# A transformer block and its gradients: one ScalarE step for two PSUM banks, and a new lead at the start

## The chip, the cores and the metric

The kernel runs on one core of one Trainium2 chip. The metric is the device time of one execution in microseconds (us). The time before is the median of three runs, 581.6 us (581.47 to 582.85). One more execution was taken with the hardware profiler; all rows of the profile come from that one.

The engines are TensorE (PE in the rows; its weight loads are PEld), VectorE (DVE), ScalarE (ACT), GpSimd (POOL) and SyncE (SP, which here issues most DMAs). Matmul results land in PSUM, which this kernel uses as eight banks of 128 partitions by 512 floats. ScalarE and VectorE take results from there to SBUF.

## The reference, cut

One block with attention and a feed-forward part, forward and backward (2048 rows, width 512, 32 heads of 16, 8 keys per row at every second position, 1792 hidden units; everything bf16). Outputs are the block's result and the gradients of x, wqkv, wo, w1, b1, w2 and b2.

```python
def _A_ref(x, wqkv, wo):                       # S=2048, D=512, H=32, Dh=16
    qkv = (x @ wqkv).reshape(B, S, 3, H, Dh).transpose(2, 0, 3, 1, 4)
    q, k, v = qkv[0], qkv[1], qkv[2]
    idx = arange(S)[:, None] - (arange(8) * 2)[None, :]      # 8 keys back, every second
    kg, vg = k[:, :, idx], v[:, :, idx]                      # [B, H, S, 8, Dh]
    logits = where(idx >= 0, einsum("bhsd,bhswd->bhsw", q, kg) * Dh ** -0.5, -1e9)
    o = einsum("bhsw,bhswd->bhsd", softmax(logits), vg)
    return o.transpose(0, 2, 1, 3).reshape(B, S, D) @ wo

def _B_ref(x, w1, b1, w2, b2):
    return gelu(x @ w1 + b1) @ w2 + b2                       # tanh form of gelu

h   = x + _A_ref(layernorm(x), wqkv, wo)
out = h + _B_ref(layernorm(h), w1, b1, w2, b2)
# outputs: out, and vjp(grad_out) for x, wqkv, wo, w1, b1, w2, b2
```

## The kernel before, in words

The 2048 rows are worked in four chunks of 512. For each chunk there are stages: `p1_ln` (first layer norm and its transposed copy `ln1T`), `p1_qkv` (projections, L804 and L821), `p1_attn` (logits and softmax), `p1_o` (attention output), `p1_h` (output projection and second norm), `p2_h`, `p2_out`, `p2_dg`, `p2_bwd` (feed-forward part, forward and backward), `p3_go`, `p3_dots`, `p3_bands`, `p3_gl1` (attention backward). At the end `wg_ffn` makes the weight gradients (L1201), sixteen accumulated matmuls for each, evicted by ScalarE and stored in pairs.

**How the order is set.** Every operation is recorded with its engine, what it reads and what it writes. A list written out in the file, `TURN`, then gives the order in which all 2029 operations are issued, and with it the order on each engine and each DMA queue. A second list, `HOMES`, gives each of the 969 buffers its PSUM bank or SBUF address. Estimated times in the code played a part only in making these lists. A real wait comes from data, or from a buffer whose place an earlier one still holds.

**The band.** The sum over the eight keys is done by `band` (L692 to L714), 64 times: in `p1_o` for the output (`ost`) and in `p3_bands` for the gradients of q, v and k (`gqs`, `gvs`, `gks`). A *pair* is two bands, m = 0 and 1. VectorE multiplies gathered rows (`R`, fetched by GpSimd's indirect DMA, L661) with transposed coefficients (`cf`, L687) into a product of 128x4096 (L698). TensorE sums it with eight matmuls into one PSUM bank (`bs`, at most two at a time, L707). ScalarE takes the bank to SBUF, turned from (d, h) to (h, d) order (L712, called *sink*). When both bands of a pair are there, `unperm` (L716 to L722) transposes the two on TensorE and ScalarE evicts the result (L564).

**The start.** x arrives in four loads of 128 rows, then weights and other chunks. `spin` (L1283) issues matmuls of zeros, eleven at the start and four behind the first transposes, `WARM = (11, 4)`. b1, 1792 biases, is loaded as 14 rows of 128 (`b1b`), turned by one TensorE transpose (`b1t`, L1306) and copied by VectorE to `b1c` (L1307). The biases are used much later by `xb` (L958). VectorE's row statistics (L577, L578), the factor `rstd` from GpSimd (L585) and `nm` (L586) give the norm (L596). The first chunk's norm is done in two halves, each followed by eight transposes (`to_fm_pairs`, L628) and one ScalarE copy. Then come the projections for k and q (two evictions each) and the first products (L672).

**Around 150 to 160 us.** ScalarE there does `xb` (L958, takes h·w1 from PSUM and adds b1), `gelu` (L961) and the squares of the gelu derivative `x2` (L976), for chunks 0 and 1 side by side, and sinks of chunk 1's and 2's attention output.

Of the kernel before, what the change touches and what calls it, by code (L numbers as in the profile page):

```python
# [427 lines left out]
def kernel(  # L428
# [114 lines left out]
    def tt_us(n, f32=False):  # L543
        return 0.16 + (1.04e-3 if f32 else 0.52e-3) * n
# [147 lines left out]
    def band(cf, R, sc, m, sgn, dst, at, sca, tag):  # L692
        pr = sb("prb" + tag, [P, 2, 4, 512], tag="prod", lim=4)
        o0 = (2 if sgn < 0 else 0) + 4 * m
        st = -1024 if sgn < 0 else 1024

        def prod():
            V.tensor_tensor(out=pr().rearrange("p a j (d h) -> p a j d h", h=H),  # L698
                            in0=_sub(R()[:, o0, 0:1], [[st, 2], [512, 4], [32, DH], [1, H]]),
                            in1=_sub(cf()[:, 2 * sc + m, 0, 0, 0:1], [[128, 2], [32, 4], [0, DH], [1, H]]), op=ALU.mult)  # L700
        op("DVE", tt_us(4096), prod, r=[R, cf], w=[pr], tag="prod" + tag)
        ps = ps_("bs" + tag, 1, "bs", 2)

        def sums():
            for hf in range(2):
                for j in range(4):
                    T.matmul(ps()[32 * j:32 * j + 32, :], lhsT=S32[:], rhs=pr()[:, hf, j, :], start=(hf == 0), stop=(hf == 1),  # L707
                             skip_group_check=True)
        op("PE", 0.45, sums, r=[CST, pr], w=[ps], tag="bsum" + tag, al=[dst])

        def out():
            A.activation(out=dst()[:, at, :].rearrange("p (h d) -> p h d", d=DH), in_=ps().rearrange("p (d h) -> p h d", h=H),  # L712
                         func=ACT.Copy, scale=sca)
        op("ACT", act_us(512), out, r=[ps], w=[(dst, at)], tag="sink" + tag)  # L714
# [71 lines left out]
    def p1_ln(c):  # L786
        xt = st_[c]["xt"]
        ln1 = sb("ln1_%d" % c, [P, TPC, D], tag="ln1", lim=L1LIM)
        layernorm(c, xt, MV1, ST1, VE1, NM1, R1, mv1, st1, ve1, nm1, rstd1, ln1, N1[c], TPC if c else 2)
        store(ln1_d[c], lambda: ln1_d[c]()[:].rearrange("(j p) d -> p j d", p=P), ln1, lambda: ln1(), 512, tag="ln1st")  # L790
        ln1T = st_[c]["ln1T"] = sb("ln1T%d" % c, [P, DC, CH], tag="ln1T", lim=L1LIM)
        (to_fm_dma if c in FM1 else to_fm if c else to_fm_pairs)(ln1, ln1T, "ln1")
        if c == 0 and WARM and WARM[1]:
            op("PE", 0.216 * WARM[1], lambda: spin(WARM[1]), r=[wz], w=[wp], tag="warm2", after=[(ln1, 3)])

# [101 lines left out]
    def p1_o(c):  # L897
# [5 lines left out]
        for sc in range(2):  # L903
            for m in range(2):
                band(cf, Rs[sc], sc, m, -1, ost, 2 * sc + m, 1.0, "o")
            unperm(ost, 2 * sc, oT, 0, sc, sc, "o")
# [226 lines left out]
    def p3_bands(c, kind):  # L1133
# [16 lines left out]
        for sc in range(2):  # L1150
            R = gather(src, sc, sgn < 0, kind, after=[(d["got"], 0)] if kind == "q" else [(cf, 0)])
            gs = sb("g%ss" % kind, [P, 2, 512], tag="gs" if c < KEEP else None, lim=4)
            for m in range(2):
                band(cf, R, sc, m, sgn, gs, m, sca, kind)
# [150 lines left out]
    pb = ps_("pb1")  # L1305
    op("PE", 0.1, lambda: T.transpose(pb.bf()[:, 0:FT], b1b[:], ident[0:FT, 0:FT]), r=[B1B], w=[pb], tag="b1t")  # L1306
    op("DVE", 0.2, lambda: V.tensor_copy(out=b1c[:], in_=pb.bf()[:, 0:FT]), r=[pb], w=[B1C], tag="b1c")  # L1307
# [216 lines left out]
N2D = ()  # L1524
B2PE = ()
GB2PE = ()
WARM = (11, 4)
GWA = ()
B1PE = ()
MD = ()  # L1530
# [44 lines left out]
```

## Time and profile before

| | us |
|---|---|
| median of three runs | 581.6 (581.47 to 582.85) |
| profiled execution | 582.24 |
| its span | 580.5 |
| mean granted TensorE clock | 0.997 |
| TensorE busy | 556.8 (96%) |
| TensorE weight loads | 261.3 (45%) |
| VectorE busy | 490.2 (84%) |
| ScalarE busy | 351.6 (61%), 517 instructions |
| GpSimd busy | 90.4 (16%) |
| ScalarE steps of band (L712), 64 in all | 592 to 606 ns each |

The span is the time between the first and the last instruction in the trace; the execution's own time has 1.74 us more. Shares of busy time are averages over the whole span; the stages differ, so the table by stage in the prediction says more. A row of the timeline reads: start, length, engine, line, operation, output and inputs by the program's names, shape, number of instructions, and in brackets how long the engine was idle before and what released it.

### The profile page before, as it was taken

How to read it: one execution, taken by the hardware profiler on the slowest of the kernel's cores; microseconds unless marked ns; L12 is line 12 of the kernel's file. 1: busy time of each engine (PE TensorE's matmuls, PEld its weight loads, DVE VectorE, ACT ScalarE, POOL GpSimd, SP SyncE). 2: the span in 40 equal slices, each digit the busy share in tenths (PEclk: the TensorE clock that was granted, in tenths of full speed). 3: DMA queues.
4: the chain of work that ended last, by engine and by line, in shares of the span. 5: the costliest groups of instructions: out<-in, count | busy, mean ns of one | idle time of the engine just before them, and what ended most of it. 6: DMA issues, size and time to landing. Idle time of an engine off the chain costs nothing.

```text
span 580.5 us, 9212 instructions
## 1 busy us (share of the span) xinstructions
PE 556.8 (96%) x3525; PEld 261.3 (45%) x3579; DVE 490.2 (84%) x645; ACT 351.6 (61%) x517; POOL 90.4 (16%) x89
## 2 busy tenths in 40 slices
PE   7999989799899999999999999999999899999997
PEld 3454544244344444444545444444444446444443
DVE  7999799999999999789865999998998899973900
ACT  5588899998997885988453424136542455364111
POOL 3020605031000000000000100432421241400000
PEclk8999999999999999999999999999999999999999
DMA  8579699999999998989999989989989996879322
GB/s 256 148 254 322 230 260 355 250 189 299 227 260 269 244 279 131 258 239 273 282 233 273 324 298 283 311 316 292 345 342 314 322 311 244 313 235 362 114 73 72
DMA packets 163147, 150.99 MB, mean 260 GB/s; under 512 B 112768, under 2 KB 149536, under 8 KB 158240
## 3 DMA queue, kind: packets, MB, share of 16 engines
q1 hardware_dynamic: 156768, 103.22, 64.1%
q0 software_dynamic: 6336, 47.19, 23.1%
q8 instruction: 28, 0.46, 0.3%
q14 instruction: 15, 0.12, 0.1%
HBM read 78.25 MB, written 42.77 MB: 208 GB/s over the span
## 4 chain that ended last, share of the span: by engine, by line
PE 75%; issue 4%; DVE 4%; ACT 3%; DMA 2%; SPq 0%; ACTq 0%; DVEq 0%
PE ps L1201 25%; PE ps L1060 8%; PE ps L1012 8%; PE ps L1173 7%; PE ps L1037 7%; PE ps L956 6%; PE ps L707 4%; PE ps L1082 2%; PE ps L722 2%; DMA gk_d<-gks 1%; PE ps L679 1%; DVE prbo L698 1%; PE ps L918 1%; ACT xb L958 1%; PE ps L650 1%
## 5 line engine op out<-in xcount | busy, mean ns | idle before, releaser
L956 PE MATMUL ps<-ln2T,w 128*128 128x512 bf16 x224 | 53.5, 379 | 2.5 <-ACT xb L958 2.3
L1037 PE MATMUL ps<-goT,w2T 128*128 128x512 bf16 x215 | 54.1, 379 | 0.4
L1012 PE MATMUL ps<-w,gl 128*128 128x512 bf16 x217 | 51.9, 379 | 0.9 <-ACT xb L958 0.6
L1201 PE MATMUL ps<-gw1in,ln2b 128*128 128x512 bf16 (+1 forms) x256 | 52.6, 353 | 0.0
L1060 PE MATMUL ps<-w1T,xb 128*128 128x512 bf16 x220 | 50.6, 379 | 0.2
L1201 PE MATMUL ps<-gor,gw2in 128*128 128x512 bf16 x217 | 50.2, 379 | 0.4 <-issue 0.2
L1039 DVE SCALAR_TENSOR_TENSOR xb<-xb,ps 128x512 bf16<-128x512 bf16 x56 | 37.9, 683 | 14.6 <-PE ps L1037 13.6
L1173 PE MATMUL ps<-wqkvT,gqkvT 128*128 128x512 bf16 x184 | 42.7, 379 | 0.6 <-issue 0.3
L958 ACT ACTIVATE xb<-ps,b1c 128x512 bf16<-128x512 f32 x56 | 36.7, 686 | 7.3 <-PE ps L956 7.2
L698 DVE TENSOR_TENSOR prbk<-Rk,cfk 128x4096 bf16<-128x4096 bf16 x16 | 36.0, 2288 | 6.0 <-DMA Rk<-q_d,rowi 2.7
L564 ACT CAST wgs<-ps 128x512 bf16<-128x512 f32 (+1 forms) x30 | 16.6, 559 | 38.8 <-PE ps L1201 38.7
L698 DVE TENSOR_TENSOR prbv<-Rv,cfv 128x4096 bf16<-128x4096 bf16 x16 | 36.3, 2287 | 3.3 <-PE ps L1201 1.8
L698 DVE TENSOR_TENSOR prbq<-Rq,cfq 128x4096 bf16<-128x4096 bf16 x16 | 36.3, 2278 | 2.3 <-PE ps L707 0.8
L672 DVE TENSOR_TENSOR prf<-qt,kt 128x4096 bf16<-128x4096 bf16 x16 | 35.9, 2278 | 1.4 <-PE ps L707 0.7
L672 DVE TENSOR_TENSOR prb<-got,vw 128x4096 bf16<-128x4096 bf16 x16 | 36.1, 2280 | 1.2 <-DMA vw<-v_d 0.6
L698 DVE TENSOR_TENSOR prbo<-Ro,cfo 128x4096 bf16<-128x4096 bf16 x16 | 36.2, 2286 | 0.3
L661 POOL DMA_INDIRECT Rq<-k_d,rowi x8 | 15.5, 1940 | 130.2 <-PE ps L1012 103.4
L737 ACT ACTIVATE gyr<-ps,rstd 128x512 bf16<-128x512 f32 x32 | 21.9, 685 | 21.5 <-PE ps L1173 18.5
L1201 PEld LDWEIGHTS <-ln2b 128*128 128x128 bf16 x256 | 24.0, 98 | 23.8 <-issue 3.4
L956 PEld LDWEIGHTS <-w 128*128 128x128 bf16 x224 | 21.1, 98 | 29.9 <-issue 5.6
L980 ACT ACTIVATE xb<-xb 128x2048 bf16<-128x2048 bf16 (+1 forms) x16 | 27.1, 1695 | 11.9 <-DVE xb L979 11.9
L1201 PEld LDWEIGHTS <-gw2in 128*128 128x128 bf16 x224 | 21.2, 98 | 27.4 <-issue 3.4
(178 smaller groups left out, 1069.8 us busy)
## 6 DMA issues: line engine op xcount, KB each, us to landing
g_d<-xrg SPq DMA_DIRECT2D x12, 512.0 KB
gh_d<-xrh SPq DMA_DIRECT2D x12, 512.0 KB
gw2in<-g_d SPq DMA_DIRECT2D x3, 2048.0 KB
gw1in<-gh_d SPq DMA_DIRECT2D x3, 2048.0 KB
ln_d<-ln SPq DMA_DIRECT2D x8, 512.0 KB
w<-in_B_w_dram SPq DMA_DIRECT2D x2, 1792.0 KB
out_dram<-wgs SPq DMA_DIRECT2D x13, 256.0 KB
v_d<-tmv SPq DMA_DIRECT2D x8, 256.0 KB
```

What stands on the lines that cost most here:

```text
L672: op("DVE", tt_us(4096), lambda g=g, pr=pr: V.tensor_tensor(out=pr(), in0=ql()[:, g, :].unsqueeze(1).to_broadcast([P, W, 512]), in1=_sub(k ...
L698: V.tensor_tensor(out=pr().rearrange("p a j (d h) -> p a j d h", h=H), in0=_sub(R()[:, o0, 0:1], [[st, 2], [512, 4], [32, DH], [1, H]]), i ...
L707: T.matmul(ps()[32 * j:32 * j + 32, :], lhsT=S32[:], rhs=pr()[:, hf, j, :], start=(hf == 0), stop=(hf == 1), skip_group_check=True)
L956: T.matmul(ps(), lhsT=w1()[:, dc, f * P:(f + 1) * P], rhs=cols(ln2T[c], dc, c in FM2), start=(dc == 0), stop=(dc == DC - 1))
L958: op("ACT", act_us(512, 1), lambda f=f, ps=ps, xb=xb, f0=f0: A.activation(out=xb()[:, f - f0, :], in_=ps(), func=ACT.Identity, bias=b1c[:, ...
L980: op("ACT", act_us(N), lambda xb=xb: A.activation(out=fl(xb), in_=fl(xb), func=ACT.Tanh, scale=GC), w=[xb], tag="tanh", mode=2)
L1012: T.matmul(ps(), lhsT=d["g"][f // 4]()[:, f % 4, j * P:(j + 1) * P], rhs=w2()[:, f, :], start=(f == 0), stop=(f == FT - 1))
L1037: T.matmul(ps(), lhsT=w2T()[:, dc, f * P:(f + 1) * P], rhs=goT()[:, dc, :], start=(dc == 0), stop=(dc == DC - 1))
L1039: op("DVE", 0.70, lambda f=f, ps=ps, z=z, f0=f0: V.scalar_tensor_tensor(out=z()[:, f - f0, :], in0=z()[:, f - f0, :], scalar=1.0, in1=ps() ...
L1060: T.matmul(ps(), lhsT=d["d"][f // 4]()[:, f % 4, j * P:(j + 1) * P], rhs=w1T()[:, f, :], start=(f == 0), stop=(f == FT - 1))
L1173: T.matmul(ps(), lhsT=d["gqkv"]()[:, b, j * P:(j + 1) * P], rhs=wqkvT()[:, b, :], start=(i == 0 and b == ks[0]), stop=(i == 2 and b == ks[ ...
L1201: T.matmul(ps()[:, 0:N], lhsT=l, rhs=r, start=(n == 0), stop=(n == k - 1))
```

## The change

Four things change together.

1. `band` becomes `bands`, which does a whole pair. The two products and the two groups of sums stay as they are, each sum in a PSUM bank of its own (at most two, as before). One ScalarE step of 128x1024 then takes both banks; the distance between the banks is a stride in its address pattern, so they need not be neighbours. 64 sinks become 32.
2. `b1t` and `b1c` are no longer recorded ahead of everything but in `p1_ln` of chunk 0, behind `ln1T`. The first rows' transposes now stand ahead of them.
3. `WARM` is (18, 4): seven more matmuls of zeros at the start.
4. `TURN` and `HOMES` are new as a whole (1997 operations). The stages follow one another as before. Most operations move by two or three us against their neighbours, some by up to 30. The weights of k are loaded ahead of those of q, q's first half is evicted ahead of k's, `b1t` stands behind six groups of projection matmuls and `b1c` ahead of the first product. Of the two squares (L976) that stood together near 153 us, one is now ahead of an earlier `gelu` and one behind a later one. At the end three pairs of rows are evicted and stored close together.

The diff, without the two lists:

```diff
-    def band(cf, R, sc, m, sgn, dst, at, sca, tag):
-        pr = sb("prb" + tag, [P, 2, 4, 512], tag="prod", lim=4)
...
+    def bands(cf, R, sc, sgn, dst, at, sca, tag):
+
+        two = []
+        for m in range(2):
+            pr = sb("prb" + tag, [P, 2, 4, 512], tag="prod", lim=4)
...
+            op("DVE", tt_us(4096), prod, r=[R, cf], w=[pr], tag="prod" + tag)
+
+            ps = ps_("bs" + tag, 1, "bs", 2)
+            two.append(ps)
...
+            op("PE", 0.45, sums, r=[CST, pr], w=[ps], tag="bsum" + tag, al=[dst])
 
         def out():
-            A.activation(out=dst()[:, at, :].rearrange("p (h d) -> p h d", d=DH), in_=ps().rearrange("p (d h) -> p h d", h=H),
-                         func=ACT.Copy, scale=sca)
-        op("ACT", act_us(512), out, r=[ps], w=[(dst, at)], tag="sink" + tag)
+            p0, p1 = two
+            A.activation(out=dst()[:, at:at + 2, :].rearrange("p m (h d) -> p m h d", d=DH),
+                         in_=_sub(p0(), [[(p1.home - p0.home) * BANK, 2], [1, H], [H, DH]]), func=ACT.Copy, scale=sca)
+        op("ACT", act_us(1024), out, r=two, w=[(dst, at), (dst, at + 1)], tag="sink" + tag)
...
+        if c == 0:
+            pb = ps_("pb1")
+            op("PE", 0.1, lambda: T.transpose(pb.bf()[:, 0:FT], b1b[:], ident[0:FT, 0:FT]), r=[B1B], w=[pb], tag="b1t", after=[(ln1T, None)])
+            op("DVE", 0.2, lambda: V.tensor_copy(out=b1c[:], in_=pb.bf()[:, 0:FT]), r=[pb], w=[B1C], tag="b1c")
...
-            for m in range(2):
-                band(cf, Rs[sc], sc, m, -1, ost, 2 * sc + m, 1.0, "o")
+            bands(cf, Rs[sc], sc, -1, ost, 2 * sc, 1.0, "o")
...
-            for m in range(2):
-                band(cf, R, sc, m, sgn, gs, m, sca, kind)
+            bands(cf, R, sc, sgn, gs, 0, sca, kind)
...
-    pb = ps_("pb1")
-    op("PE", 0.1, lambda: T.transpose(pb.bf()[:, 0:FT], b1b[:], ident[0:FT, 0:FT]), r=[B1B], w=[pb], tag="b1t")
-    op("DVE", 0.2, lambda: V.tensor_copy(out=b1c[:], in_=pb.bf()[:, 0:FT]), r=[pb], w=[B1C], tag="b1c")
...
-WARM = (11, 4)
+WARM = (18, 4)
```

More of the change, by code (lines that the diff above doesn't have):

```diff
@@ L690, in coefs, with prod, sums @@
         return cf
-    def band(cf, R, sc, m, sgn, dst, at, sca, tag):
-        pr = sb("prb" + tag, [P, 2, 4, 512], tag="prod", lim=4)
[L694 to L709, printed above, removed]
+    def bands(cf, R, sc, sgn, dst, at, sca, tag):
+        two = []
+        for m in range(2):
+            pr = sb("prb" + tag, [P, 2, 4, 512], tag="prod", lim=4)
+            o0 = (2 if sgn < 0 else 0) + 4 * m
+            st = -1024 if sgn < 0 else 1024
+            def prod(pr=pr, o0=o0, m=m):
+                V.tensor_tensor(out=pr().rearrange("p a j (d h) -> p a j d h", h=H),
+                                in0=_sub(R()[:, o0, 0:1], [[st, 2], [512, 4], [32, DH], [1, H]]),
+                                in1=_sub(cf()[:, 2 * sc + m, 0, 0, 0:1], [[128, 2], [32, 4], [0, DH], [1, H]]), op=ALU.mult)
+            op("DVE", tt_us(4096), prod, r=[R, cf], w=[pr], tag="prod" + tag)
+            ps = ps_("bs" + tag, 1, "bs", 2)
+            two.append(ps)
+            def sums(pr=pr, ps=ps):
+                for hf in range(2):
+                    for j in range(4):
+                        T.matmul(ps()[32 * j:32 * j + 32, :], lhsT=S32[:], rhs=pr()[:, hf, j, :], start=(hf == 0), stop=(hf == 1),
+                                 skip_group_check=True)
+            op("PE", 0.45, sums, r=[CST, pr], w=[ps], tag="bsum" + tag, al=[dst])
```

250 rows, old and new, of tables (HOMES, TURN) are left out of this document.

## The prediction

> **What bounds the kernel now.** I read the table of busy time by stage first, then the waits of TensorE, then the chain that ended last, then the timeline where those point.
>
> The first view is the windows table: stretch in us, its length, then busy time and count of instructions of PE, PEld, DVE, ACT and POOL, the granted clock, the DMA share and GB/s.
>
> ```profile
> 0.00:12.00 12.00, 7.77 (x33) 3.69 (x34) 8.66 (x30) 6.74 (x18) 3.98 (x22) 0.86 0.79 244
> 12.00:50.00 38.00, 37.45 (x274) 18.32 (x277) 36.47 (x53) 26.06 (x29) 5.23 (x5) 1.00 0.73 227
> ...
> 134.00:160.00 26.00, 22.99 (x117) 10.27 (x119) 25.31 (x47) 23.94 (x28) 2.52 (x2) 1.00 1.00 243
> 160.00:440.00 280.00, 278.27 (x1658) 129.39 (x1683) 248.53 (x335) 161.96 (x237) 33.71 (x28) 1.00 0.96 278
> 440.00:480.00 40.00, 37.96 (x290) 17.43 (x284) 34.59 (x22) 18.70 (x33) 14.20 (x10) 1.00 0.92 313
> 480.00:575.00 95.00, 93.86 (x591) 46.40 (x594) 58.04 (x77) 34.60 (x76) 9.40 (x4) 1.00 0.59 207
> 575.00:580.50 5.50, 1.83 (x9) 0.63 (x7) 0.00 (x0) 0.59 (x1) 0.00 (x0) 1.00 0.27 92
> ```
>
> From 160 to 440 TensorE is busy for 278.27 of 280 us: there only TensorE work counts, and the change removes none of it. Before 160 three engines are nearly full at once: VectorE has 36.47 of 38, and from 134 to 160 it has 25.31 of 26 beside ScalarE's 23.94, while TensorE has holes. Time is to be had in four places: the start, the stretch before 160, 440 to 480, and the end.
>
> The second view is TensorE's longest sum of waits (what waits, releaser: us in total, times, the longest); the third is the chain that ended last, by engine.
>
> ```profile
> PE ps L707 <- DVE prbo L698: 5.0, 6, 1.6
> ```
> ```profile
> PE 75%; issue 4%; DVE 4%; ACT 3%; DMA 2%; SPq 0%; ACTq 0%; DVEq 0%
> ```
>
> The sums over a band (L707) wait for VectorE's product, not for the ScalarE step that this change merges. ScalarE has 3% of the chain, so the 32 steps less are worth little by their number.
>
> **Part one: the start.** Timeline rows (start, length, engine, line; in brackets the idle time before and its releaser) of TensorE, VectorE and ScalarE, then the first projections and products, warm transposes, and the clock:
>
> ```profile
> 1.87 3.97 PE L1283 MATMUL ps<-wz 128*128 128x512 bf16 x11 [1.87 <-DVE wz L1284]
> 7.38 0.18 PE L1306 MATMUL ps<-ident,b1b 14*128 14x14 bf16 x1 [1.54 <-POOL rstd L585]
> 8.34 2.20 PE L628 MATMUL ps<-ident,ln 128*128 128x128 bf16 x16 [0.78 <-DVE ln L596]
> 10.33 1.66 PE L1283 MATMUL ps<-wz 128*128 128x512 bf16 x4
> ```
> ```profile
> 6.53 0.09 DVE L831 MEMSET kt<- 128x32 uint32 x1
> 7.59 0.17 DVE L1307 CAST b1c<-ps 128x14 f32<-128x14 bf16 x1 [0.98 <-PE ps L1306]
> 7.68 0.15 DVE L586 SCALAR_TENSOR_TENSOR nm<-mv,rstd 128x2 f32<-128x2 f32 x1
> ```
> ```profile
> 11.67 0.18 DVE L578 BATCH_NORM_AGGREGATE mv<-st 128x2 f32<-128x6 f32 x1
> 11.77 0.66 DVE L577 BATCH_NORM_STATS2 st<-xt 128x6 f32<-128x512 bf16 x1
> ```
> ```profile
> 9.62 1.96 ACT L564 COPY ln1T<-ps 128x1024 bf16<-128x1024 bf16 x2 [3.35 <-PE ps L628]
> ```
> ```profile
> 11.83 7.07 PE L804 MATMUL ps<-ln1T,wqk 128*128 128x512 bf16 x31
> ...
> 16.53 8.90 DVE L672 TENSOR_TENSOR prf<-qt,kt 128x4096 bf16<-128x4096 bf16 x4 [0.61 <-ACT qt L564]
> ...
> 33.99 1.06 PE L615 MATMUL ps<-ident,ln 128*128 128x128 bf16 x16
> ```
> ```profile
> 10.00:12.00 2.00, 2.00 (x11) 0.99 (x9) 1.90 (x7) 1.58 (x2) 0.00 (x0) 0.60 1.08 364
> ```
>
> VectorE stands idle 0.98 us because the copy of the bias vector (b1c) is ahead of the scaled mean (nm) in its order, and it waits for the transpose of that vector, which waits for its load. With both moved behind, nm can start when the memset is over, 6.53 + 0.09 = 6.62, or about 6.65: 7.68 − 6.65 = 1.03 us earlier. The first two rows' norms then let TensorE start its transposes at 8.34 − 1.03 = 7.31.
>
> The seven added matmuls of zeros stand right there. The first eleven end at 1.87 + 3.97 = 5.84. If the later seven take what the 31 projection matmuls take on a warm array, 7.07 / 31 = 0.228 each, they end at 5.84 + 1.6 = 7.4, just when the transposes are due, and cost nothing. If they run at half the clock, 0.46 each, they end near 9.0 and are late by 1.6.
>
> The sixteen transposes took 2.20 us where sixteen warm ones took 1.06, and the granted clock from 10 to 12 is 0.60: after the gap from 5.84 to 8.34 with one small transpose in it, TensorE had lost its clock. With zeros up to 7.4 it keeps it. So the second half of the transposes ends near 9.0 (its norms end 1.03 earlier, near 8.4, and eight warm transposes are half of 1.06), ScalarE's second copy ends near 10.2, against 9.62 + 1.96 = 11.58, and the projections start near 10.4 against 11.83. Not all of that 1.4 reaches VectorE: the moved transpose of the bias vector now follows six groups of four projection matmuls (24 × 0.228 = 5.5), and its copy is ahead of the first product on VectorE. So the first product starts near 10.4 + 5.5 + 0.2 + 0.2 = 16.3 instead of 16.53. But one pass of row statistics more (0.66 + 0.18 = 0.84) is already done ahead of it, so VectorE's work is 0.25 + 0.84 = 1.1 ahead. I take −1.1. The ends: −1.4 if VectorE follows the projections fully; −0.4 if the zeros run at half clock (projections near 11.1, product near 17.0, less the 0.84). The new order loads k's weights before q's and evicts q before k; the product needs both, so I put this at nothing. If a weight load came late here, its 512 KB would cost up to the 1.4 gained.
>
> Should the transposes stay at 2.20 for another cause than the clock, their second half would end 0.5 later, the term would be −0.6 and the forecast 580.2, inside the forecast's own range. The Trainium skill, "TensorE: Matmul & The Clock Gate", section "What's actually happening", speaks for that: it has the array throttled after an idle window of about 3.4 us, and the gap here is 2.5 us. The rows show a clock of 0.60 behind the gap, so I go by them.
>
> **Part two: one ScalarE step for two.** Means of single steps (busy us, mean ns), and two queues of such steps back to back:
>
> ```profile
> L712 ACT ACTIVATE ost<-ps 128x512 bf16<-128x512 f32 x16 | 9.2, 592 | 0.9 <-PE ps L707 0.8
> ```
> ```profile
> L564 ACT CAST tmv<-ps 128x1024 bf16<-128x1024 f32 x8 | 8.0, 1016 | 1.7 <-PE ps L821 1.7
> ```
> ```profile
> L958 ACT ACTIVATE xb<-ps,b1c 128x512 bf16<-128x512 f32 x56 | 36.7, 686 | 7.3 <-PE ps L956 7.2
> ```
> ```profile
> 112.30 1.55 ACT L712 ACTIVATE ost<-ps 128x512 bf16<-128x512 f32 x3
> ```
>
> Nothing here evicts two banks with this permutation in one step; the nearest is the strided 128x1024 eviction at 1016 ns. By means a pair saves 2 × 592 − 1016 = 168 ns. But steps that queue overlap: three took 1.55, so they start (1.55 − 0.59) / 2 = 0.48 apart, two occupy 0.96, and the merged one some 0.93: 0.03 saved. Of the 32 pairs only those before 160 lie where ScalarE is full; there are six. So the term is between 6 × 0.03 = 0.2 and 6 × 0.168 = 1.0; I take −0.5. The other 26 lie under TensorE's 278.27 of 280, where ScalarE has 161.96.
>
> **Part three: the new order around 150 to 160.**
>
> ```profile
> 153.24 2.84 ACT L976 ACTIVATE x<-xb 128x1024 bf16<-128x1024 bf16 x2
> ```
> ```profile
> 156.70 1.02 PE L956 MATMUL ps<-ln2T,w 128*128 128x512 bf16 x4 [2.35 <-ACT xb L958]
> 157.65 0.61 PE L707 MATMUL ps<-prbo,S 128*32 128x512 bf16 x8
> 158.20 1.04 PE L1037 MATMUL ps<-goT,w2T 128*128 128x512 bf16 x3
> 159.80 1.46 PE L1012 MATMUL ps<-w,gl 128*128 128x512 bf16 x6 [0.56 <-ACT xb L958]
> ```
>
> Two squares, 2.84 us, stand on ScalarE ahead of an eviction for which TensorE waits 2.35, and 0.56 more follow. In the new order one square comes before an earlier gelu and the other behind a later one. If the stall goes entirely, 2.35 + 0.56 = 2.9 are won; but the squares still have to be done on a ScalarE that is full, so mostly the stall moves to other steps. I take −0.6, nearer to none; the ends are 0 and −2.9.
>
> **Part four: 440 to 480, and the end.**
>
> ```profile
> 458.17 4.49 DVE L698 TENSOR_TENSOR prbk<-Rk,cfk 128x4096 bf16<-128x4096 bf16 x2 [2.74 <-DMA Rk<-q_d,rowi]
> ...
> 462.58 2.11 DVE L687 STREAM_TRANSPOSE cfv<-shv 128x512 bf16<-128x512 bf16 x2
> 462.71 1.05 PE L707 MATMUL ps<-prbk,S 128*32 128x512 bf16 x16 [1.66 <-DVE prbk L698]
> ```
> ```profile
> 576.87 0.59 ACT L564 CAST wgsq<-ps 128x512 bf16<-128x512 f32 x1 [2.87 <-PE ps L1201]
> ```
>
> VectorE waits 2.74 for a gather before two products. The new order fills part of that with a transpose (2.11 / 2 = 1.06), but TensorE's two sums then follow each other with less between: best −1.1, worst the 1.66 wait grown by a third, +0.6; I take +0.2. At the end one eviction (0.59) and one store follow the last matmuls now; in the new order three pairs of rows are evicted and stored close together: 0 to one eviction and a little more, +0.7; I take +0.1.
>
> **The rest.** The order and the addresses of the other buffers are new, mostly by two or three us either way. Between 160 and 440 TensorE's own work covers that (1.73 us idle of 280); if that cover went, a per cent of it would be 2.8. I put it at nothing.
>
> Sum: −1.1 − 0.5 − 0.6 + 0.2 + 0.1 = −1.9 against the profiled execution's 582.24 (span 580.5 and 1.74 around it), so 580.3. That execution lies 0.64 above the median of the runs shown; carried to the median 581.6 it is **579.7**. What can be told from no change is 0.3%, 1.74 us: faster is below 579.86, slower above 583.34.
>
> **Rivals.** First, the whole stall goes: part three is worth 2.9, so −1.9 − 2.3 = −4.2, 577.4. For it: the 2.35 is one wait with one cause. Against: ScalarE's 23.94 of 26.
>
> Second, slower: the merged step holds both banks. The limit of two banks for these sums is unchanged. Before, the first half's bank was free and half of the pair evicted while VectorE made the second product; now both banks stay occupied until one step of 1.016 after the second sums, and the next pair's sums and this pair's transposes (L722) wait behind it. By the written order about half of the 32 pairs have one or two groups of four matmuls (4 × 0.228 = 0.91 each) between the second sums and those transposes. The merged step needs 1.016 and some 0.2 on either side of it for the handovers, 1.4. With nothing ahead on ScalarE and two groups it fits; it decides where a bias eviction (0.686) stands ahead: 0.686 + 1.016 + 0.2 − 1.5 = 0.4. At 12 such pairs this is 4.8 us of TensorE time where nothing hides it: −1.9 + 4.8 = +2.9, 584.5. For it: TensorE has 278.27 of 280, so every wait there counts. Against: TensorE's waits now hold almost none on the old step. The Trainium skill, "PSUM — Partial Sum Buffer", section "Summary: rules for kernel authors", asks to evacuate promptly, which speaks against this change in the same way; no run here shows a price for it yet.
>
> Third, nothing: the lead of the start is lost where VectorE and ScalarE are both full (134 to 160), and the stall only changes its place: −0.1 to −0.5, 581.3.
>
> **Chances.** Forecast 0.45, with its own range 578.0 to 581.3 and so 0.28 of it below 579.86; first rival 0.19; second 0.24; third 0.12. Faster 0.28 + 0.19 = 0.47, same 0.17 + 0.12 = 0.29, slower 0.24. The range reaches to both rivals with the part-four ends: 577.0 to 584.6.
>
> **What would show it.** Right for part one: eighteen zeros ending near 7.4, sixteen transposes in about 1.1, clock near 1 from 10 to 12, projections from 10.4, first product near 16.3. Part two: 32 steps of 128x1024 with about 1.0 mean. Part three: a smaller sum of waits of L956 for xb, with about the same ScalarE busy time from 134 to 160. Wrong: a row of L722 or L707 waiting for ScalarE's merged step with some us in total (second rival), a first product after 17.0, or TensorE's idle time from 160 to 440 grown beyond 3 us, which would be the new order's price that I put at nothing.

## The result, and the profile after

The changed kernel takes 601.2 us (median of four runs, 597.45 to 614.09) against 582.2 for the kernel before (four runs, 581.47 to 583.18). The ratio is 1.030, with a 95% interval of 1.024 to 1.037: some 18 us slower. I had forecast 579.7 and given 0.24 to slower. Ratios here and below leave out runs that lie more than 1.5% above the fastest of the same kernel; where I give medians, all runs are in.

The profiled execution of the changed kernel took 599.57, its span is 597.8 (580.5 before). The table by stage of the changed kernel, in the columns of the prediction:

```profile
10.00:12.00 2.00, 1.76 (x13) 0.77 (x11) 1.90 (x7) 1.24 (x2) 0.00 (x0) 1.00 1.09 368
134.00:160.00 26.00, 20.14 (x106) 9.03 (x106) 20.05 (x39) 25.73 (x29) 2.13 (x2) 1.00 1.14 196
160.00:440.00 280.00, 272.90 (x1578) 126.13 (x1605) 245.39 (x342) 154.53 (x214) 24.34 (x25) 0.99 0.96 272
440.00:480.00 40.00, 36.45 (x312) 18.45 (x312) 35.17 (x20) 20.83 (x31) 11.53 (x7) 1.00 0.85 300
```

TensorE lost work at two kinds of place: 134 to 160 (20.14 busy, 22.99 before), and all through the long stretch that was full before (272.90 of 280, 278.27 before). Over the whole span it is idle for 597.8 − 561.3 = 36.5 us, against 23.7. It is also busy for 4.5 us more (561.3 against 556.8), and the seven added matmuls of zeros, 1.6 by the forecast, are only a part of that: from 159.9 to 166.7, behind the longest wait below, its granted clock is 0.50. TensorE's waits in the changed kernel say for what (what waits, releaser: us in total, times, longest):

```profile
PE ps L965 <- DMA ln2T<-ln: 9.4, 2, 8.4
PE ps L712 <- ACT ost L718: 4.1, 2, 2.5
PE ps L1209 <- ACT gvs L718: 2.9, 3, 1.1
...
PE ps L1181 <- ACT gqs L718: 1.4, 1, 1.4
PE ps L728 <- ACT gqs L718: 1.2, 1, 1.2
PE ps L1181 <- ACT gks L718: 1.1, 1, 1.1
PE ps L728 <- ACT gvs L718: 1.1, 1, 1.1
```

L718 is the merged step. All its rows together, with the smaller ones, are 14.4 us; before, waits for the same step (L712) were 0.7. The first row is one wait of 8.4 us. Of SyncE and TensorE around it (timeline of the changed kernel; SPq rows show how long SyncE needed to issue):

```profile
138.62 2.25 SPq L559 DMA_TRANSPOSE w1T<-in_B_w_dram  x1
140.97 2.40 SPq L559 DMA_TRANSPOSE xrg<-gl  x1
143.42 0.59 SPq L555 DMA_DIRECT2D out_dram<-h2s  x1
144.06 14.70 SPq L559 DMA_TRANSPOSE w1T<-in_B_w_dram  x1
158.87 2.47 SPq L559 DMA_TRANSPOSE ln2T<-ln  x1
```
```profile
163.20 1.03 PE L965 MATMUL ps<-ln2T,w 128*128 128x512 bf16 x2 [8.36 <-DMA ln2T<-ln]
```

One transposing load took 14.70 us where the other of its kind here took 2.25, and the load that TensorE needs (ln2T) stood behind it. At the same time a gather (the indirect DMA for `R`) was in flight, issued by GpSimd at 140.71. From issue to landing the gathers of this kind took, least, median and longest, first in the changed kernel and then before:

```profile
DMA to landing us min/median/max: 7.4/9.4/18.2
```
```profile
DMA to landing us min/median/max: 7.2/8.6/14.0
```

The one of 18.2 is the gather issued at 140.71; the gather at the same place of the kernel before took 7.7. So there were two suspects: the merged step and a jam of DMAs that the new order brought about. Of the waits that the kernel before had, those for VectorE's products (L707 before, L712 after) fell from 5.0 to 0.4, and that of 2.3 for `xb` went.

### The profile page after: what moved, and what is told of

Same layout as the page of the kernel before. It is cut to its first block, busy times and chain, and to the rows that moved or that the text cites. A ratio compares the mean times of both kernels' runs of the same rounds, so it can differ in the third digit from the quotient of the medians.

```text
span 597.8 us, 9178 instructions
## 1 busy us (share of the span) xinstructions
PE 561.3 (94%) x3534; PEld 263.0 (44%) x3586; DVE 491.5 (82%) x645; ACT 349.3 (58%) x485; POOL 77.1 (13%) x89
## 4 chain that ended last, share of the span: by engine, by line
PE 86%; ACT 8%; DMA 3%; issue 2%; DVE 0%; SPq 0%; POOL 0%; ACTq 0%
PE ps L1209 25%; PE ps L1021 8%; PE ps L1069 8%; PE ps L965 7%; PE ps L1181 7%; PE ps L1046 6%; PE ps L814 5%; PE ps L712 5%; PE ps L728 2%; PE ps L1091 2%; PE ps L679 2%; PE ps L927 2%; PE ps L831 2%; PE ps L650 1%; DMA ln2T<-ln 1%
## 5 line engine op out<-in xcount | busy, mean ns | idle before, releaser
L965 PE MATMUL ps<-ln2T,w 128*128 128x512 bf16 x224 | 55.2, 388 | 9.5 <-DMA ln2T<-ln 9.4
L967 ACT ACTIVATE xb<-ps,b1c 128x512 bf16<-128x512 f32 x56 | 36.5, 686 | 12.9 <-PE ps L965 12.6
L701 DVE TENSOR_TENSOR prbo<-Ro,cfo 128x4096 bf16<-128x4096 bf16 x16 | 36.3, 2286 | 9.2 <-issue 5.1
L701 DVE TENSOR_TENSOR prbq<-Rq,cfq 128x4096 bf16<-128x4096 bf16 x16 | 36.2, 2287 | 8.5 <-PE ps L1181 3.1
L701 DVE TENSOR_TENSOR prbv<-Rv,cfv 128x4096 bf16<-128x4096 bf16 x16 | 36.4, 2286 | 3.4 <-DMA Rv<-go_d,rowi 1.4
L701 DVE TENSOR_TENSOR prbk<-Rk,cfk 128x4096 bf16<-128x4096 bf16 x16 | 36.0, 2287 | 3.3 <-PE ps L712 2.7
L965 PEld LDWEIGHTS <-w 128*128 128x128 bf16 x224 | 21.5, 99 | 36.3 <-DMA ln2T<-ln 8.8
L564 ACT COPY gqkvT<-ps 128x1024 bf16<-128x1024 bf16 x24 | 23.9, 1014 | 18.8 <-PE ps L728 14.8
L1021 PEld LDWEIGHTS <-gl 128*128 128x128 bf16 x224 | 21.9, 99 | 27.2 <-issue 2.6
```

Source lines behind the costliest of these rows:

```text
L564: fn = lambda: A.copy(out=ap(), in_=pap())
L965: T.matmul(ps(), lhsT=w1()[:, dc, f * P:(f + 1) * P], rhs=cols(ln2T[c], dc, c in FM2), start=(dc == 0), stop=(dc == DC - 1))
L967: op("ACT", act_us(512, 1), lambda f=f, ps=ps, xb=xb, f0=f0: A.activation(out=xb()[:, f - f0, :], in_=ps(), func=ACT.Identity, bias=b1c[:, ...
L1021: T.matmul(ps(), lhsT=d["g"][f // 4]()[:, f % 4, j * P:(j + 1) * P], rhs=w2()[:, f, :], start=(f == 0), stop=(f == FT - 1))
```

## The experiments

All runs of one group share the runs of the kernel before on the same chip; its medians there were 582.1 (first four), 584.6, 584.3 and 584.2. Edits to the order are moves in `TURN`, with the addresses as they were unless said.

**Two suspects taken apart.** First, in the changed kernel, the slow load goes behind ln2T's:

```diff
 SyncE:  w1T, xrg, out_dram,
-        w1T, ln2T, q_d, ...
+        ln2T, w1T, q_d, ...
```

> The changed kernel with one thing moved: SyncE's last transposing load of w1T, which took 14.7 us from 144.06, stands behind ln2T's transposing load instead of ahead of it. Theory A (the load meets a gather of 128 packets of 10 KB and neither gets on; the order, not the merging, costs most): that load takes 2 to 3 us again, ln2T is issued near 151, the wait of 8.4 at L965 and the lost clock behind it go, 10 to 13 us faster than the changed kernel, 588 to 591. Theory B (the merged step costs nearly all): the stall was covered by others, at most 3 us faster, 597 to 600. Rival within A: ln2T's own transposing load meets the same gather and takes its place in the jam, then no gain.

Measured: 598.7 (595.0 to 603.7), ratio 1.027 (1.019 to 1.035). Little was won, if anything, and the gather was as slow as before: its consumer on VectorE, the product at L701, started at 157.74 (159.02 in the changed kernel). The rival within A holds: ln2T's own load, issued at 150.10, now took 7.95 us instead of 2.47, and TensorE again has one long wait at L965, 7.3 us for another input (`ga`). Moving that load alone is not enough. xrg's transposing load, issued at 140.72, still stood beside the gather; that this is the reason was a guess, which a later experiment takes up.

Second, the merged step is split again in the changed kernel, each half waiting for its own sums:

```diff
-        op("ACT", act_us(1024), out, r=two, w=[(dst, at), (dst, at + 1)], ...)
+        for m in range(2):
+            op("ACT", act_us(512), out, r=[two[m]], w=[(dst, at + m)], ...)
```

> The changed kernel with the merged ScalarE step split into two again, each waiting for its own sums, the second directly behind the first in the place of the merged one; order, addresses, start as in the changed kernel. Theory B: the waits of TensorE for L718, 14.4 us in total, nearly go: 9 to 14 us faster than the changed kernel, 587 to 592. Theory A: these waits cost 2 to 5 us by themselves because other work is behind them anyway, 596 to 599; the 14.7 us load stays.

Measured: 596.6 (591.1 to 601.3), ratio 1.027 (1.021 to 1.033). TensorE's table has no wait for L718 left, and the slow load stays, with 12.09 us. By medians 4.7 us were won, by the profiled executions 8.5 (591.1 against 599.6), by the ratios hardly anything; scatter of 10 us hides which, and this run does not decide between the two theories.

Third, both edits:

> Both of the foregoing edits in the changed kernel. If jam and merged steps are separate costs they add up: 12 to 5 us less each, 576 to 586, so with the new start and order it is at or below the kernel before. If they are the same time seen twice, it is no better than the better one of the two, 587 to 591. If the new order has a price of its own, it stays above 584.

Measured: between 588.3 and 611.5 over four runs, too scattered for a ratio. Inconclusive: the gather was still held up, with 14.2 us from issue to landing.

Fourth, merging alone, in the kernel before: `band` becomes `bands` for 28 of the 32 pairs, and seven of the sums' buffers get another bank; start and order stay.

```diff
-        for m in range(2):
-            band(cf, R, sc, m, sgn, gs, m, sca, kind)
+        bands(cf, R, sc, sgn, gs, 0, sca, kind)
```

> The kernel before with 28 of its 64 / 2 pairs merged (the other four cannot be, other buffers use their banks in between), each merged step in the place of the later one of the two, seven of the sums' buffers in another bank; start and order as before. Theory B: 28/32 of the price, 8 to 12 us slower than before, 590 to 594, with rows of L707, L722 or L1201 waiting for L712's merged step. Theory A: 2 to 5 us slower, 584 to 587. What I forecast for the merging alone: 579 to 583.

Measured: 595.1 (593.7 to 596.4), ratio 1.022 (1.018 to 1.026): 12.9 us slower, and steady. In the order of the kernel before, merging alone costs this much, which is Theory B. One of its pairs shows why, in the timelines of TensorE and of ScalarE:

```profile
359.95 1.05 PE L714 MATMUL ps<-prbv,S 128*32 128x512 bf16 x16
360.93 1.04 PE L1216 MATMUL ps<-gor,gw2in 128*128 128x512 bf16 x4
361.80 0.61 PE L615 MATMUL ps<-ident,ghr 128*128 128x128 bf16 x8
362.25 1.89 PE L1216 MATMUL ps<-gor,gw2in 128*128 128x512 bf16 x8
365.30 1.89 PE L1216 MATMUL ps<-gor,gw2in 128*128 128x512 bf16 x8 [1.16 <-ACT gvs L729]
```
```profile
362.45 1.01 ACT L564 COPY ghT<-ps 128x1024 bf16<-128x1024 bf16 x1 [1.81 <-PE ps L615]
364.23 1.02 ACT L729 ACTIVATE gvs<-ps 128x1024 bf16<-128x1024 f32 x1 [0.76 <-PE ps L1216]
```

Both groups of sums (L714, sixteen matmuls) are over at 361.00. ScalarE is free at 363.46. Yet the merged step (L729) starts only at 364.23, released by L1216, matmuls of a weight gradient that it does not read; and the next matmuls of L1216 wait for the merged step's end and lose 1.16. This pair's sums are in banks 0 and 7. The weight gradient accumulates in a bank between. It looks as if a step that reads two banks with a stride were taken, by the waits of the program, to touch everything from the first to the last.

That gives a count to test (banks from `HOMES`, waits of TensorE over 0.5 us that end with the end of a merged step). In the changed kernel the 13 pairs whose banks are one or two apart have none; of the 19 pairs three or more apart 13 have one, 0.56 to 2.48 each, 14.2 in total. In the kernel before with 28 pairs merged, of 14 pairs four or more apart 11 have one. The rule is not clean there: the four pairs three apart have none, and of the ten closer ones three have one, two neighbours (0.59 and 0.70) and a pair two apart with another buffer in use in the bank between (1.11).

**The waits between the banks.** Two kernels with the same 18 pairs merged in the kernel before, the other 14 left as two steps; only the banks differ. In the first, each merged pair has neighbouring banks, in the second, banks as far apart as were free:

```diff
 HOMES, the pair (v, 1) of chunk 1:
-    near: banks next to each other
+    far:  banks 0 and 7
```

> The kernel before with 18 of its 32 pairs merged, each of them in two neighbouring banks (19 of the sums' buffers get another bank for that), the other 14 pairs with their two steps; start and order as before. Theory C (a merged step that reads two banks that lie apart also waits for TensorE's work in the banks between them, and that work waits for it; neighbours have nothing between): no waits of TensorE for merged steps beyond 1 us in total, 581 to 583.5. Theory D (the merged step is late because it is one step of 1.02 us behind the second sums, wherever its banks are): 18/28 of what the merging of 28 pairs cost, +8, 589 to 591.

> The same 18 pairs merged in the kernel before, order and start as before, but their banks put as far apart as free banks allow (17 pairs four to seven banks apart, one neighbouring). Theory C: 10 to 15 waits of some 1.1 us of TensorE, each followed by the end of a merged step, 591 to 600. Theory D: as with neighbouring banks, within 2 us of that kernel.

Measured: neighbours 585.7 (584.1 to 587.8), ratio 1.003 (1.000 to 1.006); far apart 597.9 (595.6 to 600.2), ratio 1.024 (1.019 to 1.029). Same instructions, same order, 12 us between them; with banks far apart 12 of the 17 such pairs have a wait of over 0.5. TensorE's waits for the merged step, all of them with neighbours, and the first of eleven rows with banks far apart:

```profile
PE ps L1216 <- ACT gvs L729: 0.7, 1, 0.7
PE ps L739 <- ACT gqs L729: 0.7, 1, 0.7
PE ps L714 <- ACT gvs L729: 0.7, 1, 0.7
PE ps L650 <- ACT ost L729: 0.6, 1, 0.6
PE ps L739 <- ACT ost L729: 0.6, 1, 0.6
```
```profile
PE ps L1216 <- ACT gks L729: 2.9, 3, 1.2
...
PE ps L1216 <- ACT gvs L729: 2.3, 2, 1.2
...
PE ps L739 <- ACT gqs L729: 1.8, 2, 1.1
PE ps L739 <- ACT ost L729: 1.1, 1, 1.1
```

Theory C is right for nearly all of the cost. With neighbours there are still five waits of 0.6 to 0.7, 3.3 us in total, three times what I expected at most, and 585.7 lies above the 581 to 583.5 that I expected, with the kernel before at 584.3 in this group. This small rest may be Theory D, which is what my second rival said: the step takes 1.02 instead of 0.59 behind the second sums, where the order left room for the shorter one. That reading is not shown. Either way, these 18 merged pairs gain nothing even in neighbouring banks.

**The held-up gather.** In the changed kernel both transposing loads near the gather are moved behind ln2T's:

```diff
-SyncE:  w1T, xrg, out_dram, w1T, ln2T, q_d
+SyncE:  w1T, out_dram, ln2T, xrg, w1T, q_d
```

> The changed kernel with two transposing loads on SyncE moved behind ln2T's: that of xrg (was at 140.97) and the last of w1T (was at 144.06), so that none is in flight when the packets of the gather at 140.7 start. Theory (transposing packets of 256 B in flight at the start of a gather of 10 KB packets hold both back): the gather is over in about 7 us, no transposing load is longer than 6 us before 200, the runs lie within 4 us of each other as the kernel before does, and the time falls to what the merged steps cost: 588 to 593. Rival (the gather is slow for another reason): still a gather of over 10 us there, 595 or more.

Measured: 591.9 (590.5 to 598.8), ratio 1.015 (1.009 to 1.022); the changed kernel had 1.030. So the place of these two loads cost some 9 us. Packets in flight while the gather's own 1.31 MB were moved, in the view of DMA activity of the changed kernel (144 to 158 us), of this one (144 to 148), and of the kernel before (139 to 145):

```profile
DMA packets 1641, 1.89 MB, mean 135 GB/s; under 512 B 1270, under 2 KB 1511, under 8 KB 1511
```
```profile
DMA packets 208, 1.37 MB, mean 342 GB/s; under 512 B 32, under 2 KB 79, under 8 KB 79
```
```profile
DMA packets 453, 1.60 MB, mean 267 GB/s; under 512 B 48, under 2 KB 324, under 8 KB 324
```

Nearly all of the over a thousand small packets of the first row are those of transposing loads (256 B). Where they shared the time with the gather's 128 packets of 10 KB, all together moved 135 GB/s and the gather's packets needed some 12 us; in the other two they needed 3 to 4 us. The Trainium skill, "DMA: Bandwidth & Descriptors", section "Rules for kernel authors", says in its row on keeping transposes of different queues apart: "A transpose next to ordinary DMAs needs nothing". That row is about corrupted data and says nothing of time; next to this gather, the two loads cost time.

Both remedies together, first with all pairs split, then with 27 pairs merged in neighbouring banks:

> The same two loads moved, and the merged step split into two again. If the held-back gather and the merged step are the two causes: 577 to 583, that is no slower than the kernel before, and as steady. If the new order costs something of its own: 584 to 588, with waits of TensorE spread over many places.

> The changed kernel with the two transposing loads moved away from the gather, and 27 pairs merged in neighbouring banks (the other five with two steps). Theory C: the 8 to 10 us of waits for merged steps go, 580 to 584 at a clock of 0.997, the level of the kernel before; if the new order costs nothing by itself, 579 to 581. Theory D: as the kernel with these loads moved alone, 590 to 593.

Measured: 590.3 (581.6 to 601.9), ratio 1.002 (0.997 to 1.007), and 593.1 (583.5 to 606.5), ratio 1.004 (0.999 to 1.009). By the ratios both are at the level of the kernel before, but these rest on five of ten and five of twelve runs. With that reservation, splitting the pairs once the loads are moved wins 1.3%, some 8 us (from 1.015 to 1.002). The medians of all runs are 6 and 9 us above the kernel before and miss the ranges expected. The runs spread over 20 us and more, where those of the kernel before spread over 8: the new order is not steady even without its two large faults, and why is not shown.

Can the jam be made in the kernel before? Two additional transposing loads (a block of w1T again, the same data) go beside its gather at 137, and for comparison near 119, where there is none:

```diff
+    for tg in ("w1Tx", "w1Ty"):
+        xload(w1T, lambda i=3: w1T()[:, :, i * P:(i + 1) * P], lambda i=3: B_w1[i * P:(i + 1) * P, :], 448, key=3, tag=tg)
```

> The kernel before with two additional transposing loads of 448 KB (a block of w1T a second time, the same data), which SyncE issues behind the store of k at 137.6, so that their packets are in flight when those of the gather at 137.0 start (139.9). Theory: this gather takes 12 to 18 us instead of 7, the two loads take over 8 us together, ln2T's behind them is late, 588 to 596, and the runs scatter. Rival (the new order has another cause of its late gather): two loads cost their own 5 us of SyncE at most, the gather is over in 7 to 9 us, 582 to 585.

> The kernel before with the same two additional loads of 448 KB as in the earlier experiment, but issued behind the transposing load of xrg near 119, where no gather is in flight. If the place beside the gather was what cost: the two take 4 to 6 us of SyncE together instead of 11.9, ln2T's load near 145 is on time, 581 to 583. If the loads cost by themselves: 584 to 587 as there.

Measured: 586.7 (584.9 to 589.7), ratio 1.003 (1.000 to 1.006) beside the gather; 587.6 (585.7 to 598.7), ratio 1.006 (1.002 to 1.009) away from it. In time they cannot be told apart: two loads more cost 2 to 3 us wherever they stand, where I had expected 588 to 596 beside the gather. So this test fails to show a price of the place. The stretch from SyncE's issue of the first to its end with the second does differ, beside the gather first:

```profile
139.43 11.92 SPq L559 DMA_TRANSPOSE w1T<-in_B_w_dram  x2
```
```profile
120.48 6.77 SPq L559 DMA_TRANSPOSE w1T<-in_B_w_dram  x2
```

Both stretches hold a wait: the two loads write the same place, so the second is issued only when the first has landed, 10.4 us after its issue beside the gather and 5.3 away from it. Issuing the first took 4.31 and 1.54. The gather itself took 10.0 us there, not 12 to 18, though the small packets came about as densely beside it (620 under 512 B in 6.6 us) as in the changed kernel (1248 in 12.8). So a transposing load is held up beside a gather, by one execution of each kernel. Small packets in flight do not by themselves explain how a gather comes to be held up as badly as in the changed kernel; that is not settled.

**The start and the squares alone.** The new start in the kernel before (eighteen zeros, `b1t` and `b1c` later):

> The kernel before with the new start alone: eighteen matmuls of zeros, the bias vector's transpose behind six groups of projections and its copy ahead of the first product. My first step said 1.1 us ahead at the first products, so 580.5 to 581.5 if all of it is kept, 582 if it is lost later. Against it: no run so far shows the changed kernel ahead at 50 us, then 582 to 584.

Measured: 583.2 (580.5 to 586.5), ratio 0.998 (0.995 to 1.001).

The two squares moved in the kernel before, alone and together with the new start:

```diff
 ScalarE:
+  x2(0,3)
   gelu(1,0) ... gelu(1,1)
-  x2(0,3) x2(1,0)
   xb(1,8) gelu(1,2)
+  x2(1,0)
   xb(1,13) xb(1,12) gelu(1,3)
```

> The kernel before with only the two squares moved. Part three of the prediction: the wait of 2.35 of L956 for xb near 156 goes and part of it comes back at other steps of ScalarE or VectorE, 0 to 2.9 us faster, 579 to 582. Rival: VectorE, which needs the squares and is full there, gets them later and the stall comes back whole: 581 to 584.

> The kernel before with the new start (eighteen matmuls of zeros, the bias vector's transpose later) and the two squares moved as in the changed kernel: that of chunk 0 ahead of the first gelu of chunk 1, that of chunk 1 behind its third gelu. No merged step. If both are gains: 1.1 to 1.7 us from the start (no half-clock stretch near 8 to 12) and 0.6 to 2.9 from the squares, 578 to 580.5 where the kernel before has 581.5. If the squares only move the stall: as the start alone, 580.5 to 581.

Measured: squares 584.5 (581.3 to 589.0), ratio 1.002 (0.998 to 1.005); both 582.9 (581.0 to 585.8), ratio 0.998 (0.995 to 1.002). In the kernel with the squares alone the stall has not gone but moved, from L956 to the matmuls of L1012:

```profile
PE ps L1012 <- ACT xb L958: 2.4, 1, 2.4
```

So no version tried here is shown to be faster than the kernel before; the start alone comes nearest, and its interval still holds 1.

## Why the prediction was wrong, point by point

**The start was right in its mechanism; its size did not come through.** Zeros, transposes and projections of the changed kernel on TensorE, then the first product:

```profile
1.87 6.23 PE L1291 MATMUL ps<-wz 128*128 128x512 bf16 x18 [1.87 <-DVE wz L1292]
8.29 0.89 PE L628 MATMUL ps<-ident,ln 128*128 128x128 bf16 x8 [0.19 <-DVE ln L596]
9.61 0.62 PE L628 MATMUL ps<-ident,ln 128*128 128x128 bf16 x8 [0.44 <-DVE ln L596]
10.07 1.03 PE L1291 MATMUL ps<-wz 128*128 128x512 bf16 x4
11.33 2.97 PE L814 MATMUL ps<-ln1T,wqk 128*128 128x512 bf16 x12 [0.24 <-ACT ln1T L564]
```
```profile
16.94 2.29 DVE L672 TENSOR_TENSOR prf<-qt,kt 128x4096 bf16<-128x4096 bf16 x1
```

The transposes took 0.89 + 0.62 = 1.51 instead of 2.20 and the clock from 10 to 12 is 1.00 instead of 0.60: the zeros keep the array warm, as I had read it, and the other cause that would have kept the transposes slow was not borne out. Over all profiled executions the sixteen transposes took 1.06 to 1.51 in the nine with the new start and 1.51 to 2.20 in the seven with the old. But in this execution the zeros ended at 8.10, not 7.4, the norms came later than forecast (VectorE waited 0.88 for rows of x), and the first product started at 16.94, not 16.3. In the kernel with the new start alone it started at 16.16; over all, it started between 15.9 and 17.0 with the new start and between 15.9 and 18.1 with the old, so no lead at the product is shown. The term of −1.1 is neither shown nor excluded: the ratio of 0.998 is −1.3 us, with an interval of −3.0 to +0.4.

**Part two was wrong, by its price and by its reason.** The step itself measured as assumed, 1.02 us. I gave it −0.5. Alone, in the old order, 28 merged pairs cost +12.9; in the new order, with the loads moved, the merged pairs cost some 8. The second rival had named the right kind of loss, both banks held and TensorE waiting behind the merged step, but priced it at 12 pairs of 0.4, with a bias eviction ahead as the condition. The waits are of 0.6 to 2.5, and the condition is another: banks that lie apart, with other work in a bank between. (Its 0.2 for a handover is shown by no run either: in the kernel before ScalarE started 0.04 us after the end of the TensorE work that it waited for, and TensorE 0.05 after ScalarE's, by the medians.) What I left out of the sum is that a step with two banks in one address pattern waits for others than the writers of these two. The change says in so many words that the banks need not be neighbours; I passed over it without asking what stands in between. And "TensorE's waits now hold almost none on the old step" was no argument against the rival, because a wait that does not exist yet has no row.

**"The rest" at nothing was wrong.** I had named as cover that TensorE's own work fills 160 to 440. The jam sits ahead of that stretch, in DMA queues: the new order put two transposing loads on SyncE next to a gather on GpSimd, and the 8.4 us wait is what it costs at L965. Some 9 us by the experiment, though why the gather was held up so long stays open. TensorE's idle time from 160 to 440 grew to 7.1 us, beyond the 3 that I had named as the sign of a price of the new order: some 3.2 us of it are the end of that wait (to 163.20), and 2.3 are waits for the merged step. I had costed the moves of loads only by the engine that issues them; what else was in flight was not looked at.

**Part three was wrong as a gain.** The squares alone leave the time as it was, and the wait of 2.35 returns as one of 2.36 at L1012, as the rival in its experiment said. That this is because ScalarE and VectorE are full there is argued, not shown.

**Part four was right in small things.** VectorE's wait of 2.74 for the gather before `prbk` is gone, and behind the last eviction of the three close pairs there are 3.04 us to the end of the span, as before. Neither shows in the time.

## What to carry to other kernels

When one step is made to read two buffers through a stride, ask which buffers lie between them and who works there: give such pairs neighbouring places, and read for each wait of the new step whether its releaser writes anything that the step reads. Here a merged step saved nothing where TensorE was the bound; it also ends later than the first of the two did, so look at what stood behind that one. And when an order is written anew, lay the DMA queues over each other too: a load costed by its issue time can be held up by what another queue has in flight.

## What the runs showed of the hardware that I had not expected

The clock is lost in pieces, and not in every execution. The kernel before, over the 29 runs beside the last experiments, took 581.5 on average at a granted clock of 1.000 (five runs), 582.7 at 0.997 (five), 585.0 at 0.991 (five) and 586.4 at 0.988 (seven). In the profiled execution of the new start alone, two stretches ran at half clock; around the first, in three windows:

```profile
107.00:110.40 3.40, 1.30 (x12) 0.31 (x9) 3.40 (x3) 3.37 (x6) 0.00 (x0) 1.00 1.30 188
110.50:113.70 3.20, 3.20 (x14) 0.98 (x15) 3.06 (x9) 3.20 (x5) 0.00 (x0) 0.50 1.10 209
113.80:117.00 3.20, 3.20 (x16) 1.42 (x15) 3.13 (x6) 2.64 (x3) 0.00 (x0) 1.00 1.11 216
```

TensorE was busy for 1.30 of 3.40 us and then ran at 0.50 for the next 3.4. The profiled execution of the kernel before has the same gaps there (at 106.84, 109.04 and 111.24) and kept its clock; laid in steps of 3.41 us from the end of its own half-clock stretch at 11.61, its window there begins near 107.2, and in it TensorE was busy for 1.84 us. The Trainium skill, "TensorE: Matmul & The Clock Gate", section "What's actually happening", has a free-running window of 3413 ns that does not begin with the kernel; the trace's lengths and this difference agree with that. It also speaks of an idle window as the condition; here a window that was 38% busy was enough, and at the start a gap of 2.5 us with one small transpose in it. That fits the scatter of a few us between runs of one kernel, and an added gap of TensorE can then cost more than its own length.
